# Three-slot score bursts, with the 48-row rest of w_out in strips that they leave idle, on one Trainium2 core

## The chip, the cores and the metric

The kernel runs on one core of one Trainium2 chip. Five engines have their own instruction queues, each worked through in order: TensorE (PE), VectorE (DVE), ScalarE (ACT), GpSimd (POOL) and SyncE (SP, which here issues nearly all DMAs). The metric is the device time of one execution in microseconds; less is better.

## The reference

A sequence of 2048 tokens with 512 features goes through a layernorm, and the result xn through two branches that are added to the input.

```
xn  = layernorm(x)
A   = (32 heads of 16; token i sees keys i-255..i; softmax(q k / 4) v) @ wo
z   = gelu(xn @ w_in)                  # 2 x 688 columns
z1, z2 = z[:, :688], layernorm(z[:, 688:])
B   = (z1 * (w_sp @ z2 + b_sp)) @ w_out   # w_sp 2048 x 2048, w_out 688 x 512
out = x + A + B
```

## The kernel before

All matrices are bf16 with f32 sums in PSUM. Tokens stand in 16 blocks of 128 (t); two blocks are a J (8 of them), eight heads a G (4 of them). PSUM has eight banks of 512 f32 columns. In the second phase six are three score tiles S of two banks each, and two (pool ps_x) serve everything else in turn.

**First phase** (to about 82 us): layernorm, transposes, z with its gelu and layernorm, and nearly all of q, k and v. It is the same in both kernels, but for the loads of w_out in late_loads (line 179).

**Second phase.** Its order is written out by hand in ORDER, a list of steps that the loop at the end of the function works through. Every engine's queue gets its instructions in the order in which the steps issue them; no scheduler moves them.

- S (do_scores, line 662): one group of scores. A group has a kind: P and Q are the key blocks of a (J, G), D the corners of the window for two G. K is 16 per head, so the array is cut into four strips of 32 rows: strip s holds one pair of heads, its matmul at line 668 writes one bank, and four strips run side by side. A group takes two of the three S tiles, and ACT takes exp of each tile (1024 columns) into E (line 718) or ED (line 696).
- m (do_mask, line 729): DVE multiplies the cells at the edges of the window in E by maskY, or all of ED by maskC (line 724).
- p (pv, line 600): P times V for one (J, G), with the array cut into strips of 32 columns (line 628); DVE then transposes the result out of PSUM (line 635). n (normalize, line 638): reciprocal of the sums, product, transpose, all on DVE.
- g (g_work, line 530): 16 matmuls of 344 columns (line 537), one half of a block of w_sp @ z2; DVE adds b_sp and multiplies by z1 into u (line 543). After the second half a DMA transposes u, padded with zeros from 688 to 768 columns, into six chunks uT.
- f (f_work, line 566): the output of one block: six matmuls with the chunks of w_out (line 573; the sixth chunk has 48 rows with data and 80 of zeros) and four with wo (line 580), 512 columns each; DVE adds x (line 587), and a DMA stores it. The last block is done in two halves of 256 columns.
- q: four units of v that the first phase left over.

A number after a step, or alone, issues so many matmuls of the unit in hand. So a burst of scores stands between pieces of g and f, which use the full array.

Of the kernel before, what the change touches and what calls it, by code (L numbers as in the profile page):

```python
# [33 lines left out]
NFC = UPAD // P  # L34
PAD = 64
# [7 lines left out]
S q4 q4 S q4 q3 S 1 g8 S m 8 g2 S m 14 S p p S g n n 9 S m 7 g3 S 10 S 3 g m 6 S m 10 S p p S g  # L43
n m 16 S p p S g n n 16 S g m m 8 S n 8 f2 S m 8 S p p S f n m 10 g1 S m 8 S n 7 g3 S m 13 S p p
S f n m 10 S g m 8 S n 8 f2 S m 8 S p p S g n m 9 S m 7 g3 S n 13 S f m 10 S p p S g n m 9 S m 7
g3 S n 13 g1 S m 8 S 7 f2 S m 8 S p p S g n m 16 g1 S m n 8 S 7 g3 S m 13 S p p S g n m 16 S f m
n 6 S 4 f3 S m 7 S p p S g n m 16 g1 S m n 8 S 7 g3 S m 13 S p p S g n m 9 S m 7 f2 S n 8 S p p
S g n m 9 S m 7 g3 S m 13 S p p S f n n 6 S m 4 f3 S m 7 g1 S m 8 S n 7 g3 S m 13 S p p S f n m
6 S 4 g m 4 S n 12 S p p S g n m 9 S m 7 g m 16 g n 16 p p f n n 10 f10 f10 f10 f10
"""  # L50

@with_exitstack
def kernel(
# [43 lines left out]
    ps_x = ctx.enter_context(tc.tile_pool(name="ps_x", bufs=2, space=bass.MemoryType.PSUM))  # L97
    psum = {"f": ps_x}

    def bank(k):  # L100
        return psum[k].tile([P, 512], F32, name=f"pj_{k}", tag=k)
# [41 lines left out]
    with ExitStack() as actx:  # L143
# [166 lines left out]
        def transposes(n, xn, parts=1):  # L310
# [6 lines left out]
            for i in range(parts):  # L317
                tp = psum["f"].tile([P, w, P], BF, name="tp", tag="f")
# [210 lines left out]

    def g_work(t, j):  # L530
        if j == 0:
            us[t] = cp.tile([P, UPAD], BF, name="u")
            nc.gpsimd.memset(us[t][:, FH:UPAD], 0.0)
        u = us[t]
        gf = ps_x.tile([P, 512], F32, name="gf", tag="f")
        for c in range(NB):
# [6 lines left out]
        nc.vector.scalar_tensor_tensor(  # L543
            out=u[:, j * HALF : (j + 1) * HALF], in0=gf[:, 0:HALF],
            scalar=b_all[:, t : t + 1], in1=z1[:, t, j * HALF : (j + 1) * HALF],
            op0=ALU.add, op1=ALU.mult,
        )
# [17 lines left out]

    def f_work(t, c0):
        if c0 == 0 and t + 2 < NB:
            load_xo(t + 2)
        xo = xos[t]
        w = f_cols(t)  # L570
        fo = ps_x.tile([P, 512], F32, name="fo", tag="f")
# [13 lines left out]
        if t == NB - 1 and c0 > 0:  # L585
            least_sum()
        nc.vector.tensor_tensor(
            out=xo[:, c0 : c0 + w], in0=fo[:, 0:w], in1=xo[:, c0 : c0 + w], op=ALU.add
        )
        eng = nc.scalar if c0 else nc.sync  # L590
        eng.dma_start(out=out2[t * P : (t + 1) * P, c0 : c0 + w], in_=xo[:, c0 : c0 + w])
        if not (rows or units or later):
            check_sums()
# [6 lines left out]
    def pv(J, G):  # L600
# [4 lines left out]
        o = ps_x.tile([P, 512], F32, name="o", tag="f")  # L605
# [49 lines left out]
    groups = [(0, 0, "P"), (0, 1, "P"), (0, 0, "Q"), (0, 0, "D")]  # L655
    groups += [(0, 2, "P"), (0, 3, "P"), (0, 2, "Q")]
    for J in range(1, NJ):
        for g in range(2):
            order = [(0, "P"), (0, "Q"), (0, "D"), (1, "P"), (1, "Q")]
            groups += [(J, 2 * g + k, kind) for k, kind in order]  # L660

    def do_scores(J, G, kind):
        S = [ps_s.tile([P, 2, 512], F32, name="S", tag="S") for _ in range(2)]
        q0 = 2 * J * P
        q00 = J // 2 * 512

        def mm(s, out, g, k0, nk, qs, nq):
            nc.tensor.matmul(  # L668
                out,
                lhsT=kT[32 * s : 32 * s + 32, g, k0 : k0 + nk],  # L670
                rhs=qpad[J // 2][32 * s : 32 * s + 32, g, :, qs - q00 : qs - q00 + nq],
                start=True, stop=True,
            )

        if kind == "D":
            ED[(J, G // 2)] = late().tile([P, 32, PAD], BF, name="ED", bufs=2)
            if G == 0 and J == 0:
                load_half(0)
            if G == 2 and J + 1 < NJ:
                load_half(J + 1)  # L680
            Ed = ED[(J, G // 2)]
            for g in range(2):
                for t in range(2):
                    i = 2 * J + t
                    for strip in range(2):
                        late_q = strip == 0 or J == 0
                        k0 = i * P + P if late_q else i * P - 3 * PAD
                        q0 = i * P + PAD * late_q
                        gk = G + g + (2 * strip if J == 0 else 0)
                        for s in range(4):  # L690
                            o = S[s // 2][
# [303 lines left out]
```

## Time and profile before

| | us |
|---|---|
| median of 3 runs | 256.79 (256.06 to 256.97) |
| span of the profiled execution | 253.9 |
| PE busy | 247.4 |
| DVE busy | 203.7 |
| ACT busy | 194.3 |
| POOL busy | 20.6 |

The profile is of one execution. Its span is from the first to the last instruction that it shows; the time of a run also holds what lies around that, 2.9 us against the median here. In the views, a row of instructions has its line, engine, operation, output and inputs, shape and count. In a timeline the first column is the start within the span and the second the time to the end of the last of the row, in us. In the groups, after the bar: busy us and mean ns of one, then the idle time of that engine ahead of them and what ended it. PE's ends are modelled, and a few of its records are missing, so distances between starts are what can be trusted of it.

### The profile page before, as it was taken

The page shows a single profiled execution, that of the slowest core. Times are in us where ns is not written, and L with a number is a line of the kernel's source. Part 1 is how long each engine was busy: PE and PEld are TensorE (multiplying, and loading weights), DVE is VectorE, ACT ScalarE, POOL GpSimd, SP SyncE. Part 2 cuts the span into 40 slices and gives each one's busy share as a digit, 9 for nine tenths or more (in the row PEclk, how much of TensorE's full clock was granted, in tenths as well). Part 3 has the DMA queues.
Part 4 walks back from the last instruction along what each step waited for, and adds up shares of the span by engine and source line. Part 5 has one row for each costly group of instructions (what it writes and reads, how often), then busy time and mean ns, then how long its engine had stood idle before and what let it go on. Part 6 is the DMA issues. An engine that isn't in the chain of part 4 may idle for free.

```text
span 253.9 us, 8479 instructions
## 1 busy us (share of the span) xinstructions
PE 247.4 (97%) x3680; PEld 140.1 (55%) x3700; DVE 203.7 (80%) x428; ACT 194.3 (77%) x234; POOL 20.6 (8%) x50
## 2 busy tenths in 40 slices
PE   7999999999999999999999999999999999999994
PEld 3655555555555465565455655556466555556643
DVE  7799976974747787988888979587896898888882
ACT  3766568457367999989889989989989999999200
POOL 3231212111011230000000000000000000000000
PEclk9999999999999999999999999999999999999999
DMA  6999540029200246873847082848625676442132
GB/s 226 333 203 233 127 64 22 1 62 129 60 1 0 65 46 139 114 133 82 153 56 170 26 187 54 130 108 150 143 70 64 134 127 111 136 81 79 35 75 89
DMA packets 67081, 26.76 MB, mean 105 GB/s; under 512 B 57008, under 2 KB 65504, under 8 KB 67040
## 3 DMA queue, kind: packets, MB, share of 16 engines
q1 hardware_dynamic: 66320, 25.45, 50.9%
q8 instruction: 30, 0.49, 0.9%
q10 hardware_dynamic: 720, 0.73, 0.8%
q14 instruction: 11, 0.09, 0.1%
HBM read 8.41 MB, written 2.10 MB: 41 GB/s over the span
## 4 chain that ended last, share of the span: by engine, by line
PE 97%; issue 1%; ACT 1%; DVE 1%
PE gf L537 31%; PE zp L333 14%; PE S L668 11%; PE o L628 9%; PE fo L573 8%; PE pj_o L110 6%; PE fo L580 5%; PE pj_f L110 5%; PE pj_f L128 3%; PE pj_o L128 3%; PE heat L193 1%; PE zo L333 0%; ACT z2n L341 0%; PE tp L321 0%; DVE ot L635 0%
## 5 line engine op out<-in xcount | busy, mean ns | idle before, releaser
L718 ACT ACTIVATE E<-S 128x1024 bf16<-128x1024 f32 x124 | 116.9, 1047 | 8.9 <-PE S L668 8.7
L537 PE MATMUL gf<-z2n,wspT 128*128 128x344 bf16 x512 | 83.0, 310 | 0.0
L537 PEld LDWEIGHTS <-wspT 128*128 128x128 bf16 x512 | 46.5, 98 | 29.3 <-issue 7.9
L724 DVE TENSOR_TENSOR E<-E,maskY 128x2048 bf16<-128x2048 bf16 (+1 forms) x34 | 37.6, 1114 | 3.1 <-ACT E L718 3.1
L333 PE MATMUL zp<-w_in_sb,xnT 128*128 128x344 bf16 x224 | 36.9, 309 | 0.1
L668 PE MATMUL S<-qpad,kT 32*128 32x256 bf16 (+2 forms) x848 | 31.7, 260 | 0.6
L696 ACT ACTIVATE ED<-S 128x1024 bf16<-128x1024 f32 x30 | 29.4, 1043 | 0.5 <-PE S L668 0.5
L333 PEld LDWEIGHTS <-xnT 128*128 128x128 bf16 x224 | 21.7, 98 | 14.4 <-ACT xnT L324 0.7
L635 DVE STREAM_TRANSPOSE ot<-o 128x512 f32<-128x512 f32 x32 | 22.2, 714 | 7.4 <-PE o L628 7.4
L543 DVE SCALAR_TENSOR_TENSOR u<-gf,b_all,z 128x344 bf16<-128x344 f32 x32 | 18.3, 571 | 8.5 <-PE gf L537 8.1
L573 PE MATMUL fo<-w_out_sb,uT 128*128 128x512 bf16 (+1 forms) x91 | 23.4, 366 | 0.6 <-issue 0.2
L668 PEld LDWEIGHTS <-kT 32*128 32x128 bf16 (+1 forms) x848 | 11.1, 98 | 21.6 <-issue 20.7
L628 PE MATMUL o<-E,v_y 128*32 128x128 bf16 (+1 forms) x736 | 22.8, 239 | 0.0
L628 PE MATMUL o<-ED,vh 128*32 128x64 bf16 x960 | 21.0, 193 | 0.0
L121 DVE TENSOR_SCALAR qpad<-qt,hmask 128x512 bf16<-128x512 bf16 x32 | 9.7, 347 | 13.4 <-ACT qt L119 13.4
L110 PEld LDWEIGHTS <-wqkv 128*128 128x128 bf16 x128 | 12.5, 98 | 12.7
L341 ACT ACTIVATE z<-zp 128x688 bf16<-128x688 f32 x14 | 10.4, 743 | 10.7 <-PE zp L333 10.7
L110 PE MATMUL pj_o<-xnT,wqkv 128*128 128x512 bf16 x69 | 18.3, 379 | 0.2
L341 ACT ACTIVATE z2n<-zp 128x688 bf16<-128x688 f32 x14 | 10.4, 743 | 10.1 <-PE zp L333 10.1
L724 DVE TENSOR_TENSOR ED<-ED,maskC 128x2048 bf16<-128x2048 bf16 x15 | 18.0, 1203 | 0.0
L265 POOL TENSOR_TENSOR rs<-ve,mhalf 128x2 f32<-128x2 f32 (+1 forms) x18 | 12.1, 671 | 66.9 <-DVE ve L262 66.9
L628 PEld LDWEIGHTS <-vh 128*32 128x32 bf16 x960 | 17.2, 98 | 0.1
(80 smaller groups left out, 250.8 us busy)
## 6 DMA issues: line engine op xcount, KB each, us to landing
vh<-v_y SPq DMA_DIRECT2D x16, 140.0 KB, 3.5
xo<-in_A_x_dram SPq DMA_DIRECT2D x16, 128.0 KB, 2.7
out_dram<-xo SPq DMA_DIRECT2D x15, 128.0 KB, 2.4
wqkv<-in_A_wqkv_dram SPq DMA_DIRECT2D x1, 1536.0 KB, 8.9
xt<-in_A_x_dram SPq DMA_DIRECT2D x2, 512.0 KB, 4.5
w_in_sb<-in_B_w_in_dram SPq DMA_DIRECT2D x5, 172.0 KB, 3.8
w_out_sb<-in_B_w_out_dram SPq DMA_DIRECT2D x1, 640.0 KB, 7.1
w_in_sb<-in_B_w_in_dram ACTq DMA_DIRECT2D x3, 172.0 KB, 4.4
```

The lines of the kernel that those rows point to most:

```text
L110: nc.tensor.matmul(pt[:], lhsT=wqkv[:, c, w0 : w0 + P], rhs=xnT[:, c, t0 : t0 + 512], start=(c == 0), stop=(c == NC - 1),)
L333: nc.tensor.matmul(out, lhsT=src[:, c, t0 : t0 + P], rhs=w_in_sb[:, c, f0 : f0 + HALF], start=(c == 0), stop=(c == NC - 1),)
L341: nc.scalar.activation(out=dst.rearrange("p (j f) -> p j f", j=2), in_=zp[:, :, 0:HALF], func=ACT.Gelu_apprx_tanh, scale=rsx[n] if n < 2 e ...
L537: nc.tensor.matmul(gf[:, 0:HALF], lhsT=wspT[t][:, c, :], rhs=z2n[:, c, j * HALF : (j + 1) * HALF], start=(c == 0), stop=(c == NB - 1),)
L543: nc.vector.scalar_tensor_tensor(out=u[:, j * HALF : (j + 1) * HALF], in0=gf[:, 0:HALF], scalar=b_all[:, t : t + 1], in1=z1[:, t, j * HALF ...
L573: nc.tensor.matmul(fo[:, 0:w], lhsT=uTs[t][:, ch, :], rhs=w_out_sb[:, ch, c0 : c0 + w], start=(ch == 0), stop=False,)
L628: nc.tensor.matmul(o[32 * s : 32 * s + 32, c0 + r0 : c0 + r0 + n], lhsT=v[:, m, h * VW : h * VW + 32], rhs=rhs(s), start=(i == 0), stop=(i ...
L635: nc.vector.transpose(out=ot[:].rearrange("p b j -> p (b j)"), in_=o[:])
L668: nc.tensor.matmul(out, lhsT=kT[32 * s : 32 * s + 32, g, k0 : k0 + nk], rhs=qpad[J // 2][32 * s : 32 * s + 32, g, :, qs - q00 : qs - q00 + ...
L696: nc.scalar.activation(out=Ed[:, 16 * i : 16 * i + 16, :], in_=S[i][:].rearrange("p b (x q) -> p (b x) q", q=PAD), func=ACT.Exp, scale=SM_ ...
L718: nc.scalar.activation(out=E[(J, G)][:, b0 + 2 * i : b0 + 2 * i + 2, :], in_=S[i][:], func=ACT.Exp, scale=SM_SCALE,)
L724: nc.vector.tensor_tensor(out=v, in0=v, in1=mask.unsqueeze(1).to_broadcast([P, v.shape[1], *mask.shape[1:]]), op=ALU.mult,)
```

## The change

Scores are cut into **slots**, half a P or Q group: one S tile, two strips, one exp. do_corners does what do_scores did for D. In ORDER, S issues two slots (as before, though now they can be any two that follow each other), and the new steps A, B and T issue three, with all three S tiles. In a three-slot burst the first slot's two strips run in a first pass, the other two slots' four strips in a second.

The strips idle in the first pass take the rest of w_out: its last 48 rows are two pieces of 24 rows, and each is a matmul of one strip (rest_mm). B opens an output sum with one of its pieces, A closes one with the other, T closes one and opens the next; between, y issues the other nine matmuls (half_mm), and the sum holds one of the two banks of ps_x. ORDER has 10 A, 10 B and 2 T, so 12 output blocks are done in this way; the other four go through f_work as before, with six chunks. For this, g_work spreads the last 48 columns of u over those two of four 32-column strips that the block needs, in two or three instructions for the second half instead of one, and u is two fixed tiles, cleared only where the strips differ from those of the block two before. w_out's rest is loaded into all four strips, by four DMAs instead of one.

The third tile of a three-slot burst is copied by DVE from PSUM to its place in E, and ACT takes exp of it there, in place.

The masks of E move from DVE to POOL: after each full P or Q set two affine_selects over 8 stretches of 64 put zeros beyond the edges. The masks of ED stay on DVE (step d). m is gone.

ORDER is a new list throughout.

```diff
 ORDER = """
-S q4 q4 S q4 q3 S 1 g8 S m 8 g2 S m 14 S p p S g n n 9 S m 7 g3 S 10 S 3 g m 6 S m 10 S p p S g
...
+S q4 q2 S 2 q4 S q4 g7 D 9 S g10 S d 6 p S g5 n 11 D p p S p g7 D 5 n 3 d 1 g3 n 4 B y1 1 n y1 2
+y1 3 y1 1 y1 2 A y3 g3 y1 5 d 2 B 5 y4 1 y2 A y1 g3 y1 2 y1 11 S p p D g12 S 4 n n g6 S 10 S p p
...
-            nc.sync.dma_start(out=w_out_sb[0:48, 5, :], in_=B_w_out[640:688, :])
+            for s in range(4):
+                r0 = UFULL + s % 2 * REST
+                nc.sync.dma_start(
+                    out=w_out_sb[32 * s : 32 * s + REST, NFC - 1, :], in_=B_w_out[r0 : r0 + REST, :]
+                )
...
     def g_work(t, j):
-        if j == 0:
-            us[t] = cp.tile([P, UPAD], BF, name="u")
-            nc.gpsimd.memset(us[t][:, FH:UPAD], 0.0)
-        u = us[t]
+        u = us[t % 2]
+        if j == 0 and (t < 2 or strips_of(t) != strips_of(t - 2)):
+            nc.gpsimd.memset(u[:, UFULL:UPAD], 0.0)
...
+        f0, f1 = j * HALF, min((j + 1) * HALF, UFULL)
+        parts = [(u[:, f0:f1], gf[:, 0 : f1 - f0], z1[:, t, f0:f1])]
+        if j == 1:
...
+            parts += [(dst, src[:, a:b, :], z[:, a:b, :]) for dst, a, b in rests(u, t)]
+        for dst, src, z in parts:
+            nc.vector.scalar_tensor_tensor(
+                out=dst, in0=src, scalar=b_all[:, t : t + 1], in1=z, op0=ALU.add, op1=ALU.mult,
+            )
...
+    def rest_mm(h, s, first):
+        nc.tensor.matmul(
+            h["fo"][:], lhsT=uTs[h["t"]][32 * s : 32 * s + 32, NFC - 1, :],
+            rhs=w_out_sb[32 * s : 32 * s + 32, NFC - 1, :],
+            start=first, stop=(not first and h["pos"] == NFH),
+        )
+        h["jobs"] += 1
...
+    def do_slots(n, shut=False, open_=False):
+        some = [slots.pop(0) for _ in range(n)]
+        tiles = [ps_s.tile([P, 2, 512], F32, name="S", tag="S") for _ in range(n)]
...
+        if n == 3:
+            h = some[1][3]
+            score_mm(*mms[0].pop(0))
+            if shut:
+                rest_mm(half[0], 2 * h, False)
+            if open_:
+                new = half_open()
+                rest_mm(new, 2 * h + 1, True)
+            turns = [mms[0:1], mms[1:3]]
+        else:
+            turns = [mms]
+        for turn in turns:
+            for k in range(0, max(len(m) for m in turn), 2):
+                for m in turn:
+                    for args in m[k : k + 2]:
+                        score_mm(*args)
+        for i, ((J, G, kind, h), S) in enumerate(zip(some, tiles)):
+            b0 = 4 * (kind == "Q") + 2 * h
+            part, src = E[(J, G)][:, b0 : b0 + 2, :], S[:]
+            if i == 2:
+                nc.vector.tensor_copy(out=part, in_=src)
+                src = part
+            nc.scalar.activation(out=part, in_=src, func=ACT.Exp, scale=SM_SCALE)
+            if h == 1:
+                mask_set(J, G, kind)
...
+    def mask_set(J, G, kind):
+        b0 = 4 * (kind == "Q")
+        cells = E[(J, G)][:, b0 : b0 + 4, :].rearrange("p b (e k q) -> p (b e) k q", e=2, q=PAD)
...
+        for k, pattern, op, base, step in edges:
+            nc.gpsimd.affine_select(
+                out=cells[:, :, k, :], in_=cells[:, :, k, :], pattern=pattern,
+                compare_op=op, fill=0.0, base=base, channel_multiplier=step,
+            )
```

More of the change, by code (lines that the diff above doesn't have):

```diff
@@ L584, in f_work @@
             yield
[L585 to L593, printed above, removed]
+        f_end(t, c0, w, fo)
     E = {}
@@ L933, in attention_with_maximum @@
             nc.sync.dma_start(out=out2[bass.ds(row0, P), :], in_=xo[:])
-    masks = [x for x in groups if x[2] != "P"]
+    masks = list(corners)
     units = [(J, G) for J in range(NJ) for G in range(NG)]
@@ L961 @@
                 assert next(unit, None) is None
-    assert not (left or groups or masks or units or later or any(work.values()))
+    assert not (left or slots or corners or masks or units or later or half)
+    assert not any(work.values())
     make_flag()
```

297 lines of the change are left out of this document (188 added, 109 removed).

## The prediction, made before the changed kernel was run

> **What bounds the kernel now.** I read the page first, its busy shares and its chain, then the busy time by stage, then single bursts in the timeline of TensorE (PE).
>
> ```profile
> span 253.9 us, 8479 instructions
> PE 247.4 (97%) x3680; PEld 140.1 (55%) x3700; DVE 203.7 (80%) x428; ACT 194.3 (77%) x234; POOL 20.6 (8%) x50
> PE 97%; issue 1%; ACT 1%; DVE 1%
> ```
>
> The chain that ended last is PE's own for 97% of the span: what counts is the time that PE needs for its list. The stages say where another engine is near.
>
> ```profile
> core 0: us, PE busy (x) PEld busy (x) DVE busy (x) ACT busy (x) POOL busy (x), PEclk, DMA share, GB/s
> 82.00:130.00 48.00, 47.75 (x884) 27.02 (x889) 40.47 (x70) 45.16 (x50) 4.87 (x9) 1.00 0.56 97
> 130.00:180.00 50.00, 49.55 (x960) 27.99 (x956) 41.34 (x68) 45.74 (x49) 0.82 (x5) 1.00 0.59 114
> 180.00:234.00 54.00, 53.59 (x1191) 30.65 (x1193) 46.01 (x77) 51.72 (x57) 0.82 (x5) 1.00 0.56 109
> 234.00:253.90 19.90, 16.50 (x209) 10.19 (x209) 13.65 (x28) 2.57 (x3) 0.00 (x0) 0.99 0.25 63
> ```
>
> In the attention part, 82 to 234 us, PE is busy 150.9 of 152.0 us, so at most 1.1 us of visible waiting can be won; ScalarE (ACT) is busy 142.6 (9.4 us spare), VectorE (DVE) 127.8, GpSimd (POOL) 6.5. The granted clock is 1.00. So PE is the bound, ACT close behind it, and POOL free. But a busy PE need not be an efficient one; the timeline shows what a burst of scores costs.
>
> ```profile
> 105.27 2.51 PE L537 MATMUL gf<-z2n,wspT 128*128 128x344 bf16 x16
> 107.71 0.40 PE L668 MATMUL S<-qpad,kT 32*128 32x256 bf16 x8
> 108.03 0.35 PE L628 MATMUL o<-E,v_y 128*32 128x256 bf16 x8
> ...
> 109.34 0.23 PE L628 MATMUL o<-ED,vh 128*32 128x64 bf16 x8
> 109.50 0.43 PE L668 MATMUL S<-qpad,kT 32*64 32x128 bf16 x32
> 109.86 2.51 PE L537 MATMUL gf<-z2n,wspT 128*128 128x344 bf16 x16
> 112.30 0.40 PE L668 MATMUL S<-qpad,kT 32*128 32x512 bf16 x4
> 112.63 1.34 PE L537 MATMUL gf<-z2n,wspT 128*128 128x344 bf16 x8
> 113.90 0.40 PE L668 MATMUL S<-qpad,kT 32*128 32x256 bf16 x8
> ```
>
> ```profile
> 121.55 1.03 PE L580 MATMUL fo<-wo_sb,oT 128*128 128x512 bf16 x4
> 122.42 0.31 PE L537 MATMUL gf<-z2n,wspT 128*128 128x344 bf16 x1
> ```
>
> Only starts are used, since ends are modelled. Four 512-column matmuls take 122.42 − 121.55 = 0.87 us, 0.217 us each: one **pass**. From start to next start, 16 gf take 2.44 and 8 take 1.27: 1.17/8 = 0.146 us each, with 0.10 left over for leaving the full array. The burst at 112.30 takes 0.33 us, while its four strips run side by side and need one pass: 0.11 us more. So each **change of the array's tiling** (full, rows of 32, columns of 32) costs about 0.11 us, a round trip 0.21.
>
> **The change part by part.** PE's work, counted in the two orders of its instructions:
>
> (a) The sixth chunk of w_out, 48 rows, is a full pass now. In 12 of the 16 token blocks it becomes two matmuls of one strip each, in strips that the first pass of a three-slot burst leaves idle. 12 × 0.217 = **−2.60 us** if they run beside the scores.
>
> (b) Before, 62 bursts of two slots and 15 of corners, one pass each: 77. After, 29 of two slots, 22 of three (two passes each, the first half empty but for (a)) and 15 corners: 29 + 44 + 15 = 88. 11 × 0.217 = **+2.39 us**.
>
> (c) Fewer bursts, fewer changes of tiling: 156 before, 140 after (full and rows 124 to 102, rows and columns 30 to 30, full and columns 2 to 8). 16 × 0.11 = **−1.76 us**. The price from columns to full is shown once:
>
> ```profile
> 240.14 0.35 PE L628 MATMUL o<-E,v_y 128*32 128x256 bf16 x8
> ...
> 241.85 1.46 PE L573 MATMUL fo<-w_out_sb,uT 128*128 128x512 bf16 x5
> ```
>
> Two units of PV take 1.71 us here against 109.50 − 108.03 = 1.47 between bursts; 0.24 more, though one of the six fo matmuls has no record (x5), which is likely the first. Taken whole, it would add 3 × 0.24 = 0.7 us; I take 0.
>
> (d) Waits. PE's weight loads show one clear case of slow issue in a burst, which took 105.27 − 104.58 = 0.69 us instead of 0.33:
>
> ```profile
> 104.58 0.76 PE L668 MATMUL S<-qpad,kT 32*128 32x512 bf16 x4
> 105.27 0.32 PE L537 MATMUL gf<-z2n,wspT 128*128 128x344 bf16 x1
> ```
>
> With another order it falls elsewhere or goes. Bounds: −1.1 (all idle time goes) and the first rival's +2.2; I take **−0.3**, about this one wait.
>
> Now the other engines, which must keep beside PE.
>
> ```profile
> L718 ACT ACTIVATE E<-S 128x1024 bf16<-128x1024 f32 x124 | 116.9, 1047 | 8.9 <-PE S L668 8.7
> L724 DVE TENSOR_TENSOR E<-E,maskY 128x2048 bf16<-128x2048 bf16 (+1 forms) x34 | 37.6, 1114 | 3.1 <-ACT E L718 3.1
> L724 DVE TENSOR_TENSOR ED<-ED,maskC 128x2048 bf16<-128x2048 bf16 x15 | 18.0, 1203 | 0.0
> L643 DVE TENSOR_TENSOR on<-ot,r_all 128x256 bf16<-128x256 f32 x32 | 13.6, 425 | 1.1
> L543 DVE SCALAR_TENSOR_TENSOR u<-gf,b_all,z 128x344 bf16<-128x344 f32 x32 | 18.3, 571 | 8.5 <-PE gf L537 8.1
> L641 DVE RECIPROCAL r_all<-ot 128x16 f32<-128x16 f32 x32 | 7.1, 223 | 0.0
> L374 DVE BATCH_NORM_STATS2 st<-z2n 128x6 f32<-128x344 bf16 x32 | 14.8, 504 | 0.1
> L241 DVE BATCH_NORM_STATS2 stats<-xt 128x6 f32<-128x512 bf16 x16 | 10.9, 680 | 0.9 <-DMA xt<-in_A_x_dram 0.8
> L341 ACT ACTIVATE z<-zp 128x688 bf16<-128x688 f32 x14 | 10.4, 743 | 10.7 <-PE zp L333 10.7
> L231 ACT COPY v_y<-one 128x128 bf16<-128x128 bf16 (+2 forms) x6 | 3.4, 572 | 0.0
> ```
>
> ```profile
> masks.py:199 POOL TENSOR_SCALAR_AFFINE_SELECT ident<-ident 128x128 bf16<-128x128 bf16 x1 | 0.3, 292 | 0.1
> L215 POOL TENSOR_SCALAR_AFFINE_SELECT maskY<-maskY 128x64 bf16<-128x64 bf16 x1 | 0.2, 239 | 0.0
> ```
>
> DVE loses 34 mask products, 37.6 us, and gains 22 copies of 1024 columns and 18 more short pieces of u (50 products instead of 32). A copy of this size is not in the trace: 344 and 512 columns take 504 and 680 ns, 1.05 ns a column, so 1024 take about 1.22 us; bounds 0.68 (nothing for the columns beyond 512) and 1.36 (twice that). 22 × 1.22 = 26.8; the short pieces at the 223 ns of a 16-column instruction (no less, and no more than a piece of 344 columns, 571) add 4.0. Sum −37.6 + 26.8 + 4.0 = −7 us: DVE gets lighter. Its queue is in order: behind a copy wait the transposes of PV and the products that free the two banks of PE; 1.2 us there is what a mask product took before.
>
> POOL gains 124 selects of 512 elements (two for each of 62 masked sets) and loses 9 of 16 small memsets. 64 elements take 239 ns, 128 take 292: 0.83 ns an element, so 512 take 239 + 448 × 0.83 = 0.61 us, 76 us in all. No row has eight stretches of 64 in one instruction: if each cost a whole 239 ns, one would take 1.91. I take 0.61, as element count is the only difference that the two rows show. Then 76 us lie beside 152 us of PE. PV comes at the tightest 3.6 us of PE's list after the burst that feeds it, early and in the last unit; two exps and two selects need about 0.2 + 2.0 + 1.2 = 3.4. A few tenths may be lost there; they stand in (d)'s upper bound. Without that cover each late mask holds PE up directly.
>
> [...]
>
> ACT has the same 154 exps; 22 read the copy in SBUF. Its pitch:
>
> ```profile
> 112.73 5.61 ACT L718 ACTIVATE E<-S 128x1024 bf16<-128x1024 f32 x6 [0.78 <-PE S L668]
> ```
>
> Six end after 5.61 us, so (5.61 − 1.05)/5 = 0.91 us each. For SBUF as source the nearest row is this same exp (0 more); the far end is the copy of L231, 572 ns for at most 128 elements. From PSUM 688 columns take 743 and 1024 take 1047, 0.905 each and 120 fixed, so 128 would take 236: +0.34 us. I take 0; ACT's 9.4 spare us cover up to 0.4 each. [...]
>
> The tile of the third slot is free when DVE has copied it, 1.2 us, not after three exps, 2.7 us; the next burst waits for the first two exps, as now. The four small loads of w_out for one and the 9 memsets lie beside the first phase and on the empty POOL queue: SP issues three DMAs more in the first phase, and the matmuls that need them come only in the attention part. Cost 0; if not covered, under 0.6 us each.
>
> **Sum:** −2.60 + 2.39 − 1.76 − 0.3 = −2.27 us; span 251.6 us. The profiled execution spans 253.9, with 2.9 us around it to the median of 256.79; I subtract from the median: **254.5 us** (−0.9%). Taking the bounds of (c) and (d), faster forecasts reach from 253.7 (−1.1 for (d)) to 255.5 (+0.7 for (c), and a few tenths of PV waiting).
>
> **Rivals.** *Bursts wait for tiles.* A typical stretch from one three-slot burst to the next holds 5 or 7 fo and 6 or 4 gf matmuls: 5 × 0.217 + 6 × 0.146 + 2 × 0.217 + 0.21 = 2.61 us, or 2.75 with 7 and 4; ACT needs 3 × 0.91 = 2.73. The two are level: whatever ACT is late beyond that, PE waits. 0.1 us for each of the 22 bursts (a slower exp from SBUF, a late copy) is 2.2: 256.7, no change. For it: ACT's share, and that a burst of three needs all three tiles. Against: corners and two-slot bursts between leave it time to catch up.
>
> *POOL becomes the bound.* 124 selects in the 150 us between the first exps and the last PV saturate POOL at 1.21 us each. At 1.3 us they need 161 us, and PV waits for the rest: +11, 265 us, slower. It decides from about twice my price; the eight-stretch end (1.91) would give over 80 us more. Against: both rows lie on one line by element count.
>
> *The rests don't run beside the scores* (the change doesn't do what it says). If each first pass with rests takes a pass of its own more, 22 × 0.217 = 4.8: 259.3, slower. Against: four strips with different data take one pass at 112.30.
>
> **How the numbers follow.** Forecast 0.6 (of which 0.05 lies below 0.5%), a larger gain 0.04, waits eat it 0.15, POOL the bound 0.13, rests alone 0.08. A measurement of this kernel can tell about 0.5%, 1.3 us, from no change. Faster than 255.5: 0.55 + 0.04 = 0.59; within: 0.05 + 0.15 = 0.20; slower: 0.21. The range takes the forecast and the waits: 253.3 to 257.5, and leaves out the slower ones and the largest gains; with parts of these near its ends it holds 0.8.
>
> **What would show it.** Right: three-slot bursts from first S to next full matmul in about 0.65 us, rests started with the scores of their pass; fewer than 1 us of PE idle in the attention part; selects near 0.6 us and POOL busy some 80 us more; exps from SBUF at the pitch of the others. Wrong: PV that waits for POOL, bursts that wait for ACT or a copy, or a burst near 0.87 us. The forecast falls if a select takes over 1.2 us or an exp from SBUF over 0.1 us more than from PSUM.

## The result, and the profile of the changed kernel

The changed kernel takes **255.79 us** (median of 5 runs, 255.49 to 256.01) against 256.79 before (5 runs by now, with the same median). That is 1.0 us less by the medians; the ratio is 0.9964, with a 95% interval of 0.9951 to 0.9976, or 0.9 us less. Forecast were 2.3. It is a gain, but one within the 0.5% that the prediction set as the bound; the time lies in the range of 253.3 to 257.5. A second series of the same kernel, on another chip, gave 255.88 and 0.9973 (0.9962 to 0.9984).

The page of the changed kernel, its busy times and the chain that ended last by engine (the DMA share is the load of w_in at the start and, with 1%, `row<-low` at the end):

```profile
PE 247.7 (97%) x3712; PEld 141.3 (56%) x3712; DVE 200.1 (79%) x434; ACT 195.6 (77%) x234; POOL 105.3 (41%) x165
...
PE 92%; DMA 3%; DVE 2%; ACT 1%; issue 1%; SPq 0%; DVEq 0%
```

The spans are no help: 254.0 us here and 253.9 before. The first phase is the same code, yet the first scores start at 81.98 us in the profile of before and at 83.23 here; in the 14 profiles of the experiments they start between 82.20 and 83.60, so the profile of before is the one with the luckiest start. I therefore compare from the first score to the start of the last fo matmul, and what lies behind it; below, these two stretches are called list and tail. The changed kernel's busy time by stage, with the columns of the prediction's table:

```profile
82.00:130.00 48.00, 47.81 (x798) 26.66 (x797) 35.87 (x67) 43.90 (x49) 29.58 (x43) 1.00 0.51 97
130.00:180.00 50.00, 50.00 (x1070) 29.87 (x1068) 43.38 (x73) 46.77 (x50) 27.25 (x40) 1.00 0.64 119
180.00:234.00 54.00, 53.92 (x1075) 30.82 (x1074) 45.48 (x80) 49.77 (x53) 28.72 (x46) 1.00 0.62 109
```

From 130 to 180 us PE is busy 50.00 of 50.00. GpSimd works 85.6 us between 82 and 234, 79.0 more than before, VectorE (DVE) 124.7 instead of 127.8, ScalarE (ACT) 140.4 instead of 142.6. Nobody has become the bound. A three-slot burst in the changed kernel's timeline of PE, the counterpart of the bursts that the prediction read:

```profile
113.26 0.28 PE L761 MATMUL S<-qpad,kT 32*128 32x256 bf16 x1
113.26 0.39 PE L638 MATMUL fo<-w_out_sb,uT 32*128 32x512 bf16 x1
113.27 0.60 PE L761 MATMUL S<-qpad,kT 32*128 32x256 bf16 x7
113.80 0.39 PE L662 MATMUL fo<-wo_sb,oT 128*128 128x512 bf16 x1
```

The rest of w_out (L638, 32 rows) starts in the same hundredth of a microsecond as the scores of the first pass, and the next full matmul follows 113.80 − 113.26 = 0.54 us after the first score. A burst of two slots takes 0.33. The difference, 0.21, is one pass: the rest costs nothing there. Of the 22 three-slot bursts, the 20 with one rest take 0.54 us each (0.578 the longest).

The other engines' new work, in the changed kernel's groups by line (after the bar: busy us, mean ns):

```profile
L840 ACT ACTIVATE E<-S 128x1024 bf16<-128x1024 f32 x102 | 97.6, 1027 | 9.1 <-PE S L761 9.0
...
L855 POOL TENSOR_SCALAR_AFFINE_SELECT E<-E 128x512 bf16<-128x512 bf16 x124 | 86.3, 721 | 68.0 <-ACT E L840 64.8 <-POOL E L855 3.2
...
L838 DVE CAST E<-S 128x1024 bf16<-128x1024 f32 x22 | 26.7, 1213 | 2.2 <-PE S L761 2.2
L840 ACT ACTIVATE E<-E 128x1024 bf16<-128x1024 bf16 x22 | 23.4, 1063 | 0.8 <-DVE E L838 0.6
...
L862 DVE TENSOR_TENSOR ED<-ED,maskC 128x2048 bf16<-128x2048 bf16 x15 | 19.2, 1278 | 0.0
...
L742 DVE TENSOR_TENSOR on<-ot,r_all 128x256 bf16<-128x256 f32 x32 | 16.9, 528 | 1.1
```

Selects (L855) take 721 ns on the mean, copies (L838) 1213, exps from SBUF (`E<-E`) 1063 against 1027 from PSUM. On products (L742) have gone from 425 to 528 ns, though nothing about them was changed.

**Where the time went.** From the first score to the last fo is 250.40 − 81.98 = 168.42 us before and 250.21 − 83.23 = 166.98 after (the last four fo matmuls start 0.109 us apart), −1.44. From there to the end of the span it is 3.45 before and 3.81 after, +0.36. Sum −1.08, and the timed runs say −0.9. To see what waiting is in it, I took every distance between two starts of PE and subtracted what the same pair of instructions takes elsewhere in the trace (where a matmul has no record, its pass was taken off too):

| waits of PE above 0.03 us | before | after |
|---|---|---|
| second burst of scores (84 to 85 us) | 0.14 | 0.57 |
| to 105 us | 0.61 | 0.36 |
| 105 to 240 us | 0.00 | 0.18 |
| last PV (242 us) | 0.00 | 0.28 |
| sum | 0.75 | 1.39 |

Without waits, 168.42 − 0.75 = 167.67 and 166.98 − 1.39 = 165.59: PE's list has become 2.08 us shorter, and 0.64 of it went into new waits, 0.36 into the tail.

The largest wait, in the changed kernel's timeline of PE and then of ACT:

```profile
83.23 0.40 PE L761 MATMUL S<-qpad,kT 32*128 32x512 bf16 x4
83.56 1.47 PE L161 MATMUL pj_f<-wqkv,xnT 128*128 128x512 bf16 x6
84.96 0.39 PE L761 MATMUL S<-qpad,kT 32*128 32x512 bf16 x2
85.53 0.39 PE L761 MATMUL S<-qpad,kT 32*128 32x512 bf16 x2 [0.19 <-ACT E L840]
```

```profile
83.07 1.28 ACT L516 ACT_TABLE_LOAD   x1
...
84.48 3.75 ACT L840 ACTIVATE E<-S 128x1024 bf16<-128x1024 f32 x4
```

Two slots need two of the three tiles. The second burst at 84.96 finds one tile free and waits with its other half until the first exp is done, at 85.53 (the view's 0.19 is less than the 0.57 by starts, since PE's ends are modelled). That exp could not start before 84.48, since ACT loaded its table for 1.28 us from 83.07. The order before put eight v matmuls between these bursts, the new one six (L161, x6): 0.43 us less cover. With eight, in the timeline of PE of the kernel before, the second burst takes 84.61 − 84.14 = 0.47 us, 0.14 more than the usual 0.33:

```profile
84.14 0.54 PE L668 MATMUL S<-qpad,kT 32*128 32x512 bf16 x4
84.61 0.60 PE L128 MATMUL pj_f<-wqkv,xnT 128*128 128x512 bf16 x2
```

The next is the last PV, in PE's timeline of the changed kernel, and what it waits for in DVE's:

```profile
242.69 0.23 PE L727 MATMUL o<-ED,vh 128*32 128x64 bf16 x8
243.01 0.35 PE L727 MATMUL o<-E,v_y 128*32 128x256 bf16 x8
```

```profile
242.17 0.70 DVE L602 SCALAR_TENSOR_TENSOR u<-gf,b_all,z 128x296 bf16<-128x296 f32 x2 [0.40 <-PE gf L588]
243.00 0.72 DVE L734 STREAM_TRANSPOSE ot<-o 128x512 f32<-128x512 f32 x1
```

The second unit of PV starts at 243.01, though the first issued its last matmuls at 242.69: its bank is the one that u's products read until 242.87, and u's second half is now two instructions. Finally the tail, in DVE's timeline, first of the kernel before and then of the changed one:

```profile
245.60 0.69 DVE L753 SCALAR_TENSOR_TENSOR ok<-r_all,ok 128x512 bf16<-128x512 f32 x1
...
249.96 0.26 DVE L765 TENSOR_REDUCE low<-row 1x1 f32<-1x128 f32 x1
250.71 0.42 DVE L587 TENSOR_TENSOR xo<-fo,xo 128x256 bf16<-128x256 f32 x1 [0.49 <-PE fo L580]
```

```profile
247.85 0.69 DVE L874 SCALAR_TENSOR_TENSOR ok<-r_all,ok 128x512 bf16<-128x512 f32 x1
...
250.68 0.28 DVE L886 TENSOR_REDUCE low<-row 1x1 f32<-1x128 f32 x1 [0.83 <-DMA row<-low]
250.88 0.40 DVE L627 TENSOR_TENSOR xo<-fo,xo 128x256 bf16<-128x256 f32 x1
```

Sums of P are checked at the end: a count from each partition goes through a DMA (`row`), a reduction (`low`) takes the least of these, and that makes a flag that the kernel reads last. The check is issued behind the first output block after the last normalize. Before, that is at 245.60, 4.8 us ahead of the last fo; in the new order at 247.85, 2.4 us ahead. So `low` waits 0.83 us for its DMA, and the last addition of x stands behind it: 0.67 us after the last fo's start, where before it was 0.31.

### The profile page after: what moved, and what is told of

Its sections match the earlier page's. It is cut to its first block, busy times and chain, and to the rows that moved or that the text cites. A ratio compares the mean times of both kernels' runs of the same rounds, so it can differ in the third digit from the quotient of the medians.

```text
span 254.0 us, 8684 instructions
## 1 busy us (share of the span) xinstructions
PE 247.7 (97%) x3712; PEld 141.3 (56%) x3712; DVE 200.1 (79%) x434; ACT 195.6 (77%) x234; POOL 105.3 (41%) x165
## 4 chain that ended last, share of the span: by engine, by line
PE 92%; DMA 3%; DVE 2%; ACT 1%; issue 1%; SPq 0%; DVEq 0%
PE gf L588 31%; PE zp L370 14%; PE S L761 11%; PE fo L662 10%; PE o L727 9%; PE pj_o L143 6%; PE pj_f L143 5%; PE pj_o L161 3%; PE pj_f L161 2%; DMA w_in_sb<-in_B_w_in_dram 2%; DMA row<-low 1%; DVE xo L627 1%; PE fo L680 1%; PE zo L370 0%; PE fo L687 0%
## 5 line engine op out<-in xcount | busy, mean ns | idle before, releaser
L855 POOL TENSOR_SCALAR_AFFINE_SELECT E<-E 128x512 bf16<-128x512 bf16 x124 | 86.3, 721 | 68.0 <-ACT E L840 64.8
L840 ACT ACTIVATE E<-S 128x1024 bf16<-128x1024 f32 x102 | 97.6, 1027 | 9.1 <-PE S L761 9.0
L588 PE MATMUL gf<-z2n,wspT 128*128 128x344 bf16 x512 | 88.4, 310 | 0.0
L588 PEld LDWEIGHTS <-wspT 128*128 128x128 bf16 x512 | 47.4, 98 | 30.9 <-issue 5.9
L761 PE MATMUL S<-qpad,kT 32*64 32x128 bf16 (+2 forms) x848 | 32.0, 259 | 0.2 <-ACT E L840 0.2
L602 DVE SCALAR_TENSOR_TENSOR u<-gf,b_all,z 128x344 bf16<-128x344 f32 (+3 forms) x50 | 20.4, 438 | 11.7 <-PE gf L588 11.5
L838 DVE CAST E<-S 128x1024 bf16<-128x1024 f32 x22 | 26.7, 1213 | 2.2 <-PE S L761 2.2
L840 ACT ACTIVATE E<-E 128x1024 bf16<-128x1024 bf16 x22 | 23.4, 1063 | 0.8 <-DVE E L838 0.6
L761 PEld LDWEIGHTS <-kT 32*64 32x64 bf16 (+1 forms) x848 | 12.9, 99 | 18.6 <-issue 16.4
L862 DVE TENSOR_TENSOR ED<-ED,maskC 128x2048 bf16<-128x2048 bf16 x15 | 19.2, 1278 | 0.0
```

What stands on the lines that cost most here:

```text
L588: nc.tensor.matmul(gf[:, 0:HALF], lhsT=wspT[t][:, c, :], rhs=z2n[:, c, j * HALF : (j + 1) * HALF], start=(c == 0), stop=(c == NB - 1),)
L761: nc.tensor.matmul(out, lhsT=kT[32 * s : 32 * s + 32, g, k0 : k0 + nk], rhs=qpad[J // 2][32 * s : 32 * s + 32, g, :, qs - q00 : qs - q00 + ...
L838: nc.vector.tensor_copy(out=part, in_=src)
L840: nc.scalar.activation(out=part, in_=src, func=ACT.Exp, scale=SM_SCALE)
L855: nc.gpsimd.affine_select(out=cells[:, :, k, :], in_=cells[:, :, k, :], pattern=pattern, compare_op=op, fill=0.0, base=base, channel_multi ...
```

## The experiments

My theory after the comparison: steps (a) to (c) of the sum are right, the failing step is (d), waits, with the tail that no step had; the waits are those of the beginning and the end of the second phase, where the order gives less cover. Rivals: GpSimd's selects and VectorE hold each other up; or PE's list is not what the sum says, and copies or rests cost something. Each kernel below is the changed one with an edit; the ratio is to the kernel before on the same chip, and list and tail are of its one profile. The control is the changed kernel again: its list of 167.15 beside the 166.98 above shows how far two profiles of one kernel can differ.

| kernel | median us | ratio (95%) | list | tail |
|---|---|---|---|---|
| control (no edit) | 255.88 | 0.9973 (0.9962 to 0.9984) | 167.15 | 3.83 |
| early_table | 255.70 | 0.9962 (0.9948 to 0.9977) | 167.32 | 3.82 |
| early_check | 255.46 | 0.9965 (0.9952 to 0.9977) | 168.40 | 3.46 |
| three_waits | 255.41 | 0.9959 (0.9945 to 0.9973) | 167.48 | 3.45 |
| start_as_before | 256.94 | 1.0003 (0.9976 to 1.0031) | 168.38 | 3.81 |
| wsp_first | 256.09 | 0.9990 (0.9968 to 1.0011) | 167.49 | 3.83 |
| start_wsp | 256.74 | 1.0006 (0.9977 to 1.0036) | 168.37 | 3.82 |
| start_wsp_low | 256.81 | 1.0006 (0.9979 to 1.0034) | 168.44 | 3.77 |
| start_dve0 | 256.16 | 0.9993 (0.9979 to 1.0006) | 168.36 | 3.82 |
| dve_masks_no_copy | 303.77 | 1.1858 (1.1813 to 1.1902) | 210.77 | 6.00 |
| no_copy | 260.40 | 1.0172 (1.0144 to 1.0200) | 171.49 | 4.28 |
| rest_full | 257.50 | 1.0047 (1.0031 to 1.0063) | 169.31 | 3.82 |
| start_dve_late | 255.56 | 0.9967 (0.9953 to 0.9982) | 167.13 | 3.82 |
| no_selects | 255.33 | 0.9952 (0.9932 to 0.9971) | 166.72 | 3.76 |

### The sum itself: rest_full, no_copy

**rest_full** puts the 48 rows back into one full matmul at the head of the block's other nine:

```diff
-            if shut:
-                rest_mm(half[0], 2 * h, False)
...
+        if pos == 0:
+            nc.tensor.matmul(
+                h["fo"][:], lhsT=uTs[t][:, NFC - 1, :], rhs=w_out_sb[:, NFC - 1, :],
+                start=True, stop=False,
+            )
```

> The rest of w_out is one full-array matmul of 128 rows at the head of the other nine of its block, instead of two strips in the idle part of the score bursts; all else as in the changed kernel. Theory (a rest beside the scores is free, a full pass costs 0.217 us): 12 x 0.217 = 2.6 us more than the changed kernel, 258.1 to 258.7 against 255.8. Rival (the rests cost part of a pass where they stand, by their weight loads or by strips that don't run side by side): under 1.5 us more, below 257.3.

The list grows by 169.31 − 166.98 = 2.33 us. The burst without rests takes 0.54 us as well, in this kernel's timeline of PE:

```profile
129.35 0.61 PE L761 MATMUL S<-qpad,kT 32*128 32x512 bf16 x8
129.89 0.39 PE L657 MATMUL fo<-w_out_sb,uT 128*128 128x512 bf16 x1
```

129.89 − 129.35 = 0.54, then the full rest (L657). Bursts are 3 ns shorter on the median (22 × 0.003 = 0.07), and 0.15 us of small waits are gone, so 12 passes cost 2.33 + 0.22 = 2.55 against 12 × 0.217 = 2.60. Timed, the ratios 1.0047 and 0.9964 lie 0.0083 apart, 2.1 us, and their intervals don't meet. Step (a) holds; the rival that rests cost part of a pass is out. The time, 257.5, is 0.6 under what I expected.

**no_copy** takes the third exp straight from PSUM:

```diff
-            if i == 2:
-                nc.vector.tensor_copy(out=part, in_=src)
-                src = part
```

> The third tile's exp reads PSUM directly, with no copy by VectorE. Theory (the copy frees the tile about 1.5 us earlier, and bursts need all three tiles): some bursts wait for the third tile, up to 0.1 us in each of 22, 256.3 to 258. Rival (the next burst comes late enough for three exps, and each exp is 0.04 us cheaper and VectorE 26 us lighter): no change or up to 0.4 us less than the changed kernel, 255.3 to 255.9.

The list grows by 4.5 us. One burst in no_copy's timeline of PE:

```profile
142.24 0.39 PE L761 MATMUL S<-qpad,kT 32*128 32x512 bf16 x1
...
142.92 0.39 PE L761 MATMUL S<-qpad,kT 32*128 32x256 bf16 x6 [0.18 <-ACT E L837]
143.24 0.39 PE L662 MATMUL fo<-wo_sb,oT 128*128 128x512 bf16 x1
```

From first score to the next full matmul is 1.00 us instead of 0.54: the second pass at 142.92 waits for ACT, that is for the third tile, whose exp is the last of three. Ten three-slot bursts and one of corners wait 0.26 to 0.63 us in this way, 4.8 us together. I had allowed up to 0.1 in each; the copy is worth twice my upper end. VectorE's 26.7 us for copies buy 4.5 us of PE.

### The masks: dve_masks_no_copy, no_selects

**dve_masks_no_copy** leaves out the copies and makes every mask of E a product on DVE, issued where the selects were:

```diff
-        for k, pattern, op, base, step in edges:
-            nc.gpsimd.affine_select(
...
+        nc.vector.tensor_tensor(
+            out=v, in0=v, in1=mask.unsqueeze(1).to_broadcast([P, 8, 2, PAD]), op=ALU.mult,
+        )
```

> All masks of E as products on VectorE as in the kernel before, but right behind the exps of the set, and the third exp straight from PSUM without a copy; GpSimd has no selects. Theory (contention with GpSimd costs little in all, and VectorE has room): on products back at 0.42 us from 0.53, the time equal to the changed kernel's within 0.5 us, 255.3 to 256.3. Rival (the move to GpSimd and the copies are needed for the three-slot bursts): VectorE waits in order for the exps, u and the PV results behind it come late and PE waits over 1 us in all, 257 or more.

The rival holds, far beyond its number: 303.77 us. Its groups by line (after the second bar the idle time of the engine just before, and what ended it):

```profile
L588 PE MATMUL gf<-z2n,wspT 128*128 128x344 bf16 x512 | 88.3, 309 | 9.7 <-DVE u L602 4.8 <-DVE ot L734 3.8 <-DVE xo L627 0.9
...
L851 DVE TENSOR_TENSOR E<-E,maskY 128x1024 bf16<-128x1024 bf16 x62 | 42.8, 690 | 58.1 <-ACT E L837 57.9
...
L727 PE MATMUL o<-E,v_y 128*32 128x256 bf16 x256 | 18.6, 276 | 16.5 <-DVE xo L627 9.0 <-DVE u L602 7.3
```

DVE is busy only 42.8 us with the 62 products, but stands idle 58.1 us in front of them, waiting for exps; behind each stand u, the transposes of PV and the additions of x, and PE waits for these (`<-DVE u`, `<-DVE xo`). The kernel before had the step m to put a mask later in the queue; GpSimd, with nothing else queued, needs no such place. My theory had counted busy time and not what queues behind the wait. no_copy differs from this kernel only in the masks, so these alone make about 40 us: the lists differ by 210.77 − 171.49 = 39.3 us, the medians by 43, and the granted clock was 0.97 to 0.99 in these runs against 1.00 in those of no_copy.

**no_selects** leaves the 124 selects out altogether, so the cells beyond the window's edge keep their exps:

```diff
-            if h == 1:
-                mask_set(J, G, kind)
```

> The changed kernel with its 124 selects on GpSimd left out: the cells beyond the window's edge keep their exps, nothing else is changed. Theory (what selects and VectorE take from each other is hidden, and the late selects make PE wait nowhere): on products at 0.43 us on the mean instead of 0.53, first S to last fo within 0.2 us of the changed kernel's 166.98, the time 255.5 to 256. Rival (late masks or a slowed VectorE are behind the waits of 0.64 us more than before): these waits go, 255.0 to 255.3.

The groups by line of no_selects:

```profile
L860 DVE TENSOR_TENSOR ED<-ED,maskC 128x2048 bf16<-128x2048 bf16 x15 | 18.0, 1200 | 0.0
...
L742 DVE TENSOR_TENSOR on<-ot,r_all 128x256 bf16<-128x256 f32 x32 | 13.6, 425 | 1.1
```

On products are back at 425 ns from 528, the corner products at 1200 from 1278. So it is the selects that slow them, 3.3 + 1.2 us of DVE in all. The list is 166.72, 0.26 under the changed kernel's (I had said 0.2), the ratio 0.9952 against 0.9964 with intervals that overlap. The waits near 200 us are gone, and that of the last PV falls from 0.28 to 0.19 us; together that is the 0.26. The one at 85 us is as before. Near 98 us PV no longer waits, but the burst behind it does, and the stretch from the corners' first score to the next gf matmul takes 2.47 us with and without selects. So the masks on GpSimd cost PE about a quarter of a microsecond; the rest of (d) is something else. The time, 255.33, lies between what the theory and the rival had.

### The waits one by one

**early_table** asks for the exp table before the last units of k instead of after them:

```diff
+            if n == NB - 1:
+                nc.scalar.activation(out=warm[:, 0:4], in_=warm[:, 4:8], func=ACT.Exp)
...
-                nc.scalar.activation(out=warm[:, 0:4], in_=warm[:, 4:8], func=ACT.Exp)
```

> The exp table is loaded before ScalarE's last three casts of the first phase, not after them. Theory: the second burst of the changed kernel waits 0.57 us because its second tile needs the first exp, and that follows the table load; with the load earlier the first exp starts about 0.7 us earlier, the burst waits under 0.2 us, and the time falls by 0.4 to 0.6 us against the changed kernel. Rival: the casts that now come later hold up TensorE's banks by as much, no change (within 0.2 us).

Two stretches of this kernel's timeline of PE:

```profile
83.40 0.40 PE L762 MATMUL S<-qpad,kT 32*128 32x512 bf16 x4 [0.34 <-ACT kT L149]
```

```profile
103.69 0.61 PE L589 MATMUL gf<-z2n,wspT 128*128 128x344 bf16 x3 [0.70 <-DMA wspT<-in_B_w_sp_dram]
```

The second burst no longer waits. In its place the first burst waits 0.34 us for the cast of kT, which now stands behind the table; that lies ahead of the list. And at 103.69 the third block of w_sp arrives late: 0.7 us of waiting for a DMA by the view, 0.87 by the starts, which the changed kernel doesn't show. Without it the list would be 166.45, 0.53 shorter than the changed kernel's. The edit is not likely its cause: early_check, the next kernel, changes nothing ahead of the last blocks and has such a wait too (below).

**early_check** issues the check of the sums behind the last normalize, ahead of the output block:

```diff
+            if not (rows or units or later):
+                check_sums()
```

> The check of the sums is issued right behind the last normalization, one output block earlier. Theory: the last output no longer waits for the row of sums, the final addition starts 0.3 to 0.4 us earlier after TensorE's last matmul, and the time falls by 0.3 us. Rival: the store of the last block sets the end anyway, no change.

In early_check's timeline of PE:

```profile
103.30 1.19 PE L588 MATMUL gf<-z2n,wspT 128*128 128x344 bf16 x7 [0.55 <-DMA wspT<-in_B_w_sp_dram]
...
248.83 0.81 PE L680 MATMUL fo<-w_out_sb,uT 128*128 128x256 bf16 x6 [0.31 <-DVE xo L627]
```

The tail is back at 3.46. But the check's products now stand ahead of the addition that frees a bank, and PE waits at 248.83 (0.31 us by the view, 0.48 by the starts). The rest of its longer list is the wait for w_sp at 103.30, 0.71 us by the starts. From issue to landing that load took 7.2 us here and 7.3 in early_table, against 5.6 in the changed kernel's first profile and 5.2 in the control's, so this wait comes and goes from one execution to the next. How often, a few profiles can't tell.

**three_waits** makes both edits and masks the last Q set slot by slot, with four selects of half the size:

```diff
+            if (J, G, kind) == (NJ - 1, NG - 1, "Q"):
+                mask_set(J, G, kind, 2 * h, 2)
+            elif h == 1:
```

> Both edits, and the last masked set is masked slot by slot (four selects of 256 elements), so that its second half follows its exp at once. Theory: the three waits of 0.57, 0.36 and 0.28 us go, and the time is 1.0 to 1.2 us below the changed kernel, about 2.1 us below the kernel before, near the 2.27 us that I had forecast. Rival (waits move instead of going): under 0.5 us below the changed kernel.

The last PV waited as before (0.28 us), so the mask of a whole set at once isn't its cause. The second burst's wait and the longer tail are gone, but 0.34 us stand ahead of the first score, 0.51 at the load of w_sp and 0.48 ahead of the last block. 255.41 is among the lowest here, and better than the kernel before (0.9959), but it can't be told from the changed kernel.

The **control**, the changed kernel run again beside these three:

> The changed kernel once more, beside the three that follow, on their chip. Theory: TensorE's list got 2.0 us shorter as summed, but waits inside the attention part grew by about 0.6 us against before and the last output waits 0.36 us for the row of sums; so 0.9 to 1.1 us faster than before. Rival (part of the first result is chance in the first phase, whose first w_in loads landed 1.1 us later in the changed kernel's profile): anything from 0.5 to 2 us faster.

Its ratio, 0.9973, is 0.7 us less than before, a little under what I expected; its waits are those of the first profile.

**start_as_before** restores the first three bursts' distances:

```diff
-S q4 q2 S 2 q4 S q4 g7 D 9 S g10 ...
+S q4 q4 S q4 q3 S 1 g7 D 9 S g10 ...
```

> Only the first steps of the order are those of before: eight matmuls of v stand between the first two bursts instead of six, seven instead of six behind the second. Theory: the second burst's third tile needs the first exp, which ends at the same time in any case (the table load precedes it), so the 0.57 us and 0.10 us of waiting shrink to under 0.2 us, while the list stays as long; 0.4 to 0.6 us below the changed kernel. Rival: bursts and exps are a chain that ScalarE bounds here, the wait moves on to a later burst; under 0.2 us.

The second burst waits 0.14 us again, as in the kernel before, and the 0.10 behind the next is gone; but a larger wait comes. start_as_before's timeline of all engines:

```profile
96.01 3.89 POOL L855 TENSOR_SCALAR_AFFINE_SELECT E<-E 128x512 bf16<-128x512 bf16 x6
96.17 3.22 DVE L742 TENSOR_TENSOR on<-ot,r_all 128x256 bf16<-128x256 f32 x1
...
99.78 0.53 DVE L602 SCALAR_TENSOR_TENSOR u<-gf,b_all,z 128x344 bf16<-128x344 f32 x1
...
100.37 0.29 PE L727 MATMUL o<-E,v_y 128*32 128x256 bf16 x4 [1.59 <-DVE u L602]
```

Six selects run in a row from 96.01, and an on product that needs 0.42 us alone takes 3.22 beside them. u's product comes at 99.78, and the second PV waits 1.59 us for the bank that it reads.

**start_dve0** keeps this start and gives the masks of the first two blocks back to DVE as products (step m), so that no selects run there:

```diff
-S q4 q2 S 2 q4 S q4 g7 D 9 S g10 S d 6 p S g5 n 11 D p p
+S q4 q4 S q4 q3 S 1 g7 D m 9 S g10 S d 6 p S g5 m n 11 D p p
```

> The start of the order of the kernel before, and the masks of the first two P and Q sets as products on VectorE at places of their own, so that GpSimd has no run of six selects beside VectorE's on products there. Theory (selects and on products that lie side by side hold each other up, so that u comes late): the on product of 3.2 us and the PV wait of 1.6 us at 100 us are gone, and the first S to the last fo takes 0.6 to 1.0 us less than in the changed kernel, 254.8 to 255.3 us against its 255.8. Rival (VectorE is simply late there, whoever else works): the two mask products of 1.1 us delay u as much, the wait stays above 1 us, 256.3 to 257.

DVE's timeline of start_dve0:

```profile
97.79 0.69 DVE L859 TENSOR_TENSOR E<-E,maskY 128x1024 bf16<-128x1024 bf16 x1 [0.60 <-ACT E L840]
...
98.68 0.42 DVE L742 TENSOR_TENSOR on<-ot,r_all 128x256 bf16<-128x256 f32 x1
...
99.51 0.53 DVE L602 SCALAR_TENSOR_TENSOR u<-gf,b_all,z 128x344 bf16<-128x344 f32 x1
```

The on product takes 0.42 again, but the wait stays at 1.3 us: the last mask product waited until 97.79 for its exp, and u stood behind it until 99.51. Contention was a cause in start_as_before; with it gone, the order of DVE's queue does the same. **start_dve_late** moves that one product behind u:

```diff
-... S 1 g7 D m 9 S g10 S d 6 p S g5 m n 11 D p p
+... S 1 g7 D m3 9 S g10 S d 6 p S g5 m2 n 11 m1 D p p
```

> As start_dve0, but the last of the six mask products of the first two blocks stands behind u's second half in VectorE's queue instead of ahead of it. Theory (in start_dve0 that product waited for its exp until 97.8 us and u stood behind it): the PV wait falls from 1.3 us to under 0.5, the first S to the last fo from 168.4 to about 167.5 us, the time to 255.1 to 255.5 (0.996 of the kernel before). Rival (VectorE has too much to do there in whatever order): the wait stays above 1 us and the time at 256.

start_dve_late's timeline of DVE, then of PE:

```profile
97.46 0.53 DVE L602 SCALAR_TENSOR_TENSOR u<-gf,b_all,z 128x344 bf16<-128x344 f32 x1
97.92 0.68 DVE L859 TENSOR_TENSOR E<-E,maskY 128x1024 bf16<-128x1024 bf16 x1
```

```profile
98.65 0.24 PE L727 MATMUL o<-E,v_y 128*32 128x128 bf16 x4 [0.27 <-DVE E L859]
```

u comes at 97.46 and the mask product at 97.92; PV waits for that product only, and the wait falls to 0.48 us by the starts; the list to 167.13. The theory holds. But the kernel as a whole is where the changed one was (0.9967 against 0.9964): the wait at 85 us is down to 0.14, and 0.48 us stand at 98.

**wsp_first** issues the load of the third block of w_sp ahead of the transposing DMA of the first u; **start_wsp** adds the start of before, **start_wsp_low** also the last addition ahead of `low`:

```diff
+            if t == 0:
+                load_wsp(t + 2)
             nc.sync.dma_start_transpose(out=uTs[t][:], in_=u[:])
-            if t + 2 < NB:
+            if 0 < t < NB - 2:
                 load_wsp(t + 2)
```

> For the first block alone, the load of the third block of w_sp stands ahead of the transposing DMA of u in the SP queue. Theory: in three of five profiles TensorE waited 0.5 to 0.9 us for this load, as the new order needs it about 8 us after the buffer is free, 4 us earlier than the order before; the load is issued 1.2 us earlier, the wait is 0 in every profile, and the median falls by 0.3 to 0.5 us against the changed kernel. Rival: the wait was chance of single profiles, no change within 0.2 us.

> Both edits. Theory: they add up, 0.7 to 1.1 us below the changed kernel, 1.7 to 2.1 below the kernel before. Rival: under 0.5 us below the changed kernel.

> Both edits, and the last addition of VectorE stands ahead of the minimum that waits for the row of sums. Theory: the final addition starts 0.36 us earlier, and if the store of the last block sets the end, 0.3 us are won beyond the two edits. Rival: the flag, which then comes 0.1 to 0.2 us later, sets the end: 0 to 0.2 us lost.

None is faster than the changed kernel. wsp_first has no wait for w_sp, but most other profiles have none either. With the load first, the transposing DMA of u starts 1.3 us later (counted from the first score), the first rest starts 0.10 us behind the scores of its burst at 103.82, and a unit of PV at 99.55 waits about 0.24 us; the trace doesn't show for what. With the start of before, the list is 168.4 as in start_as_before. The last addition ahead of `low` leaves the tail at 3.77: the flag, then, is as late as the addition was.

## Why the prediction was wrong

The direction and the mechanism of PE's list were right, the size was not: −0.9 us where −2.3 was forecast. The step that failed is (d), the waits, and with it the tail, for which the sum had no term.

- **(a) to (c), right.** −2.60 + 2.39 − 1.76 = −1.97 us forecast for PE's list, −2.08 found without waits. rest_full gives (a) by itself, 2.55 against 2.60. A three-slot burst takes 0.54 us; "about 0.65" in the last part of the prediction counted a change of tiling once more. The columns-to-full price that I left out of (c) is indeed none: from the last PV matmul to the first full one takes 0.13 us, no more than from PV to scores (0.12 to 0.13).
- **(d) waits, the step that failed.** Forecast −0.3, found +0.64 (0.75 to 1.39). I took the one slow burst at 104.58 as lost time that would go, and it went; I did not follow the new order's beginning, where the first steps of the two orders show the cover: six v matmuls instead of eight before the second burst, beside a table load of 1.28 us. That alone is +0.43, and two runs show it: early_table, which has the table earlier, has no wait there, and start_as_before, with eight again, has the old 0.14. The last PV adds 0.28; by the trace it waits for u's second half, two instructions of 0.70 us now where one took 0.58, which I costed on DVE as busy time (4.0 us) and not as a later release of a bank. No run undid that split; without selects this wait is 0.19. The selects' share of the whole is about 0.26.
- **The tail, not in the prediction.** +0.36: moving the normalizes towards the end moves the check, and its DMA's wait stands ahead of the last addition; early_check, with the check earlier, has the tail of before (3.46), though it loses 0.48 us ahead of the last block. The prediction named what stood behind new instructions, not what the new order had moved close to the end.
- **The other engines, right.** A select took 0.66 us when no on or corner product of VectorE ran beside it (79 of 124), 0.61 forecast, and not 1.91; beside them 0.83 on the mean, so that all 124 took 86.3 us and not 76. A copy took 1.213, forecast 1.22. DVE's −7 us became −3.6 (203.7 to 200.1), as products run slower beside selects (4.5 us); the short pieces of u added 2.1 us of busy time (18.3 to 20.4), 4.0 forecast. The exp's price from SBUF is in ACT's timeline of the changed kernel:

```profile
110.96 1.94 ACT L840 ACTIVATE E<-S 128x1024 bf16<-128x1024 f32 x2 [0.17 <-PE S L761]
112.78 1.06 ACT L840 ACTIVATE E<-E 128x1024 bf16<-128x1024 bf16 x1
113.73 1.94 ACT L840 ACTIVATE E<-S 128x1024 bf16<-128x1024 f32 x2
```

  From PSUM two exps start (112.78 − 110.96)/2 = 0.91 us apart; behind the one from SBUF the next starts after 113.73 − 112.78 = 0.95 (the median of the 22 is 0.96). The prediction took 0 for this; it is 0.04 to 0.05 us each, about 1 us over the 22, and ACT, busy 140.4 of the 152 us between 82 and 234, had room for it.
- **The rivals.** Bursts that wait for tiles did not come with the copy in place: between 105 and 240 us all waits are 0.18 us. no_copy shows how near that rival was: with the third tile free only after its exp, eleven bursts wait 4.8 us together. POOL as the bound did not come either (105.3 of 254 us busy). POOL was held up by VectorE all the same, for which the price of 0.61 us had nothing: a select beside on or corner products took up to 1.70 us.

What stays open: the waits of the second phase's first 20 us are 0.93 us in the changed kernel and 0.63 in start_dve_late, in different places. No order tried removes them together, and whether one could, I can't say from these runs. The two repairs together (three_waits) could not be told from the changed kernel in time, so that the shortfall is made of these waits rests on the traces. It is open how often the third block of w_sp comes late in the new order. Nor is it settled why the first phase of the profile of before was a microsecond quicker to the first score than most others.

## What to carry to other kernels

A list of PE's passes and changes of tiling gave the change of the steady stretch to about a tenth of a microsecond here (−1.97 us forecast, −2.08 found without waits); where an order is written anew, the loss is at its beginning, its end and the last chain to a flag or store, so walk those instruction by instruction, with what covers each wait. A wait that is removed there can come back one step later, so test a repair by the whole time, not by the wait that is gone; and before a new wait is put down to an edit, see whether a kernel that was not changed there shows it too. An engine whose queue held nothing else proved the right place for work that must wait: 62 short products that wait for exps cost about 40 us in the queue of a busy engine (dve_masks_no_copy against no_copy), the same masks on an idle one 0.3 (the changed kernel against no_selects).

## What the runs showed of the hardware

VectorE and GpSimd held each other up more than I had expected, and in both directions. In the changed kernel, selects of 512 elements took 0.66 us with no on or corner product beside them, and beside these 0.83 on the mean and up to 1.70; on products took 0.528 us on the mean, against 0.425 before and in no_selects, and, in start_as_before, beside six selects in a row, one took 3.22 us, most of the 3.89 us of the whole row. What stood behind that product in VectorE's queue waited as long: u's product started at 99.78, 3.61 us after the on product.
